# Moving weight stores and stage A's stores to the GpSimd queue, and dropping eight reloads of w_out

## The chip, the cores and the metric

The kernel runs on one core of a Trainium2 chip. The metric is the device time of one execution in microseconds (us). Engines are named as the profile names them: PE is TensorE, DVE is VectorE, ACT is ScalarE, POOL is GpSimd, and SP is SyncE, which here does nothing but issue DMA transfers. POOL, too, does nothing in this kernel but issue DMAs, apart from four tiny constants at the start.

## The reference

The input `x` has 8 batches of 3008 positions and 256 features, in float32. The first half is a real Fourier transform along the 3008 positions, a complex 256 by 256 mixing matrix with a bias, a soft threshold (lambda 0.01) and the inverse transform. The second half is a gated feed-forward layer on the resulting 24064 tokens, 256 to 2048 to 256 features.

```python
X = np.fft.rfft(x, axis=1)
Yr = Xr @ w_r - Xi @ w_i + b_r ;  Yi = Xr @ w_i + Xi @ w_r + b_i
Y = sign(Y) * max(|Y| - 0.01, 0)          # real and imaginary part apart
y = np.fft.irfft(Y, n=3008, axis=1)
h = y @ w_in ;  g = h * sigmoid(1.702 * h) ;  out = g @ w_out
```

[...]

## The kernel before

**The transform.** 3008 is 64 times 47, so each transform is done in two stages of small matrix products, stage A over 47 points and stage B over 64, joined through scratch tensors in device memory (`s1`, `s2`). For each batch, stage A has 16 steps: load a strip of `x` (line 325, tiles `xa` or `xr`), one matmul (line 342), ACT copies the result out of PSUM into a tile `aev` (line 357), and a DMA stores it to `s1` (line 358). Stage B has 12 steps: load from `s1` (lines 370 and 371, `kr` and `br`), matmuls (388), the mixing products (402 to 407), bias and threshold on DVE and ACT, four small transfers that regroup the result (427, `yr<-mv`), the inverse product (434), a copy (436, `iev`) and a store to `s2` (437). Tokens are then read back (467, `ur`) and transposed into `y` by a last product (475). Batch 0 runs first and alone. Batches 1 and 2 run their stage A as filler between the first steps of the feed-forward layer; from batch 3 on the transform of a batch is paced along it.

**The feed-forward layer.** Tokens go in 24 tiles (22 of 1024, then 2 of 768), each through 8 blocks of 256 hidden units; one tile and one block make a step, numbered n. A float32 product is three PE passes over a high and a low half (lines 147 to 149, `mm3`), made by `split` (line 144: an ACT copy and a DVE subtraction). The products are done in a Strassen scheme with seven products instead of eight: the up-projection from the start, the down-projection from the third tile on (n = 16). The first two tiles use plain `w_out` blocks (`wo`).

**The weights.** `fetch` (line 215, POOL's queue) loads a 512 KB float64 block. `from_float64` turns it into a float32 `a` and a float32 remainder `e`, with two ACT instructions (lines 230 and 234) and five DVE instructions (231, 232, 233, 235, 236). For the plain blocks, `turn(0, q)` splits that into the pair `wo[q][:, 0]` and `wo[q][:, 1]` (lines 254 to 256). `combine` (lines 259 to 276) makes the seven Strassen factors of a block. `keep` (lines 278 to 288) stores the finished factors to scratch tensors (`kept`, `kept_o`, `kept_d`), from which every later tile reloads them: `wq<-kept` at line 298, `wd<-kept_d` at line 652.

The eight Strassen factors of `w_out` are made in the steps n = 5 to 12. Each of these steps fetches the raw block of `w_out` a second time and converts it a second time, because the first conversion has been split by then.

**What sets the order.** The code is traced in program order; a planner then simulates the engines and decides the order of each engine's instructions and the reuse of buffers. Each engine works through its own list in order, so an instruction that waits holds up everything behind it on that engine or DMA queue. `tc.issue_after` puts an instruction behind a given one on the same engine. Buffers come in rings: tag `g` (13 slots) holds `xa`, raw weights, the converted pair `wae` and the factors `w`; tag `w2` (7 slots) holds `aev`, `xr`, `br`, `iev`, `mv` and most `ur`. A load into a ring slot waits until the slot's last user is done; for a slot that held `aev` that is the landing of its store.

Of the kernel before, what the change touches and what calls it, by code (L numbers as in the profile page):

```python
# [9 lines left out]
F32 = mybir.dt.float32  # L10
# [102 lines left out]
def fourier_mix_then_gated_ffn(ctx: ExitStack, tc: tile.TileContext, x, w_r, w_i, b_r, b_i, w_in, w_out, pack, kbs, out):  # L113
    nc = tc.nc
# [78 lines left out]
    kept = [dw.tile([128, 2 * NP * 128], F32, name=f"kept{q}") for q in range(NQ)]  # L193
    kept_o = [dw.tile([128, 4 * 256], F32, name=f"kept_o{q}") for q in range(NQ)]
    kept_d = [dw.tile([128, NP, 2, NQ // 2, 128], F32, name=f"kept_d{h}") for h in range(2)]
    up_w, wo, fresh = {}, {}, []
# [16 lines left out]
    def fetch(kind, q):  # L213
        raws[kind, q] = r = slot4([128, 2, 256], I64, "wraw")
        nc.gpsimd.dma_start(r, source(kind, q))

    def from_float64(kind, q):
        if (kind, q) not in raws:
            fetch(kind, q)
        raw = raws.pop((kind, q))  # L220
        ae = slot4([128, 2, 2, 256], I32, "wae")
        a, e = ae[:, 0], ae[:, 1]
        m = buf([128, 2, 256], F32, "wm", tag="s", bufs=3)
        af, ef = a.bitcast(F32), e.bitcast(F32)
        v = nc.vector

        def word(dt, w):
            return raw.bitcast(dt).rearrange("p c (f w) -> p c f w", w=2)[:, :, :, w]

        nc.scalar.activation(ef, word(F32, 1), AF.Abs)  # L230
        v.tensor_scalar(ef, ef, TINY, None, ALU.max)
        v.tensor_scalar(a, e, 3, 0x3FFFFFF8, ALU.logical_shift_left, ALU.bitwise_and)
        v.scalar_tensor_tensor(a, word(I32, 1), -0x40000000, a, ALU.bitwise_and, ALU.bitwise_or)
        nc.scalar.activation(m, word(U32, 0), AF.Copy, scale=2.0 ** -52)
        v.tensor_scalar(e, a, -0x800000, None, ALU.bitwise_and)
        v.tensor_tensor(ef, ef, m, ALU.mult)
        return af, ef
# [21 lines left out]
    def combine(kind, q, a, e, wq):  # L259
        a, e = (t.rearrange("p c (f n) -> p c f n", f=2) for t in (a, e))  # L260
        v = nc.vector
        t = slot4([128, 8, 128], F32, "w8")
        a11, a12, s4, n22, s1, s2, s3, a21 = (t[:, i] for i in range(8))
        v.tensor_tensor(t[:, 0:2], e[:, :, 0], a[:, :, 0], ALU.add)
        v.tensor_tensor(a21, e[:, 0, 1], a[:, 0, 1], ALU.add)
        v.scalar_tensor_tensor(n22, e[:, 1, 1], -1.0, a[:, 1, 1], ALU.mult, ALU.subtract)
        v.tensor_tensor(s1, a21, n22, ALU.subtract)
        v.tensor_tensor(s3, a21, a11, ALU.subtract)
        v.tensor_tensor(s2, s1, a11, ALU.subtract)
        v.tensor_tensor(s4, a12, s2, ALU.subtract)  # L270
        if kind:
            split(wq[:, 0], wq[:, 1], t[:, 0:7])
        else:
            wq = [slot4([128, NP, 128], F32R, "wq_d") for _ in range(2)]
            split(*wq, t[:, 0:7])
        fresh.append((kind, q, wq))

    def keep(n):
        for kind, q, wq in [f for f in fresh if f[0] != 1 or f[1] <= n]:
            fresh.remove((kind, q, wq))  # L280
            with tc.issue_after(stored[-1]):
                if kind == 1:
                    nc.sync.dma_start(kept[q], wq.bitcast(F32).rearrange("p h a n -> p (h a n)"))
                elif kind == 2:
                    nc.sync.dma_start(kept_o[q], wq.bitcast(F32).rearrange("p h f n -> p (h f n)"))
                else:
                    for h in range(2):
                        nc.sync.dma_start(kept_d[q // 4][:, :, h, q % 4], wq[h].bitcast(F32))

    def load_wo(q):  # L290
        wo[q] = buf([128, 2, 2, 256], F32R, "wo", tag="wd", bufs=WD)
# [12 lines left out]
    def spectral(b, s2):  # L304
# [34 lines left out]
        def stage_a(q):  # L339

            ps = bank()
            ins = nc.tensor.matmul(ps[:96], lhsT=ka32, rhs=xs.pop(q), start=True, stop=True).ins  # L342
            if plain_a:
                done_a.append(ins)
            if plain and q < 4:
                if q == 0:
                    shared.append(buf([96, 4, 512], F32, "aev_y", tag="y", bufs=1))
                ev = shared[0][:, q]
            elif plain and q < 7:
                if q == 4:  # L350
                    shared.append(buf([96, 3, 512], F32, "aev_t", tag="gl", bufs=JIT))
                ev = shared[1][:, q - 4]
            elif plain and q < 11:
                ev = buf([96, 512], F32, "aev_s", tag="s", bufs=3)
            else:
                ev = buf2("aev")[:96].rearrange("p j d -> p (j d)")
            evacuated.append(nc.scalar.copy(ev, ps[:96]).ins)
            mine.append(nc.sync.dma_start(s1w[:, 512 * q:512 * (q + 1)], ev).ins)
            stored.append(mine[-1])

        def load_b(sp):
# [466 lines left out]
    for n in range(NT * NQ):  # L828
        k, q = divmod(n, NQ)
        load_up(n + 2)  # L830
        last = q == NQ - 1 and k + 1 < NT
        if last:
            coming = Tile(k + 1)
        starts = list(np.cumsum((0,) + groups(k)))
        if k < PLAIN:
            group = None
        elif q in starts:
            group = (Group if k + 1 < NT else PlainGroup)(cur, q, groups(k)[starts.index(q)])
        if n == NQ * PLAIN + 1:
            wo.clear()  # L840
        step = Step(cur, q, group)

        if not queue and nextb < NB:
            if nextb == 2:
                queue = queue2
            else:
                first, second, *_ = spectral(nextb, new_s2(nextb))
                queue = first + [(4000, lambda: None)] + second
            nextb += 1
            total = None  # L850
        if queue and total is None and not filler:
            total, spent, n0 = sum(c for c, _ in queue), 0.0, n
            n1 = NQ * S * (nextb - 1) // TILE - 9
        for i, p in enumerate(PATTERN + (0,) * (k < PLAIN)):
            if p:
                step.up(p)
                if last:
                    coming.factor(p)
            elif behind:
                behind.pop(0)()  # L860
            else:
                for _ in range(2 if k + 1 == NT and q >= 4 else 1):
                    down()
            if i == 0 and n + EARLY < NQ:
                fetch(0, EARLY + n)
            if i == 4 and n + EARLY < NQ:
                with tc.issue_after(gelu[-1]):
                    turn(0, EARLY + n)
            if i == 5 and n + WQ < NQ:
                fetch(1, WQ + n)  # L870
            if i == 9 and n + WQ < NQ:
                with tc.issue_after(gelu[-1]):
                    turn(1, WQ + n)
            q2 = (n - 5) if 5 <= n < 5 + NQ else None
            if i == 0 and q2 is not None:
                fetch(0, q2)
            if i == 9 and q2 is not None:
                with tc.issue_after(gelu[-1]):
                    combine(0, q2, *from_float64(0, q2), None)
            if i % 5 == 2:  # L880
                fill(2)
                if i in (2, 12):
                    keep(n if i == 2 else -1)
                if preload_b and len(filler) <= 12:
                    preload_b()
                    preload_b = None
            part = n + (i + 1) / len(PATTERN)
            while queue and total and spent < total * (part - n0) / (n1 - n0):
                c, do = queue.pop(0)
                spent += c  # L890
                do()
            need = base[k + 1] + (base[min(k + 2, NT)] - base[k + 1]) * min(1.0, max(0.0, (part - NQ * k - 2.5) / 4))
            if JP * done < need:
                while queue and need + JP > S * (nextb - 1):
                    queue.pop(0)[1]()
                tokens_to(need)
        for do in behind:
            do()
        behind = []
        if group is None:  # L900
            behind = [lambda f=f, h=h, m=m, step=step: step.down(f, h, m) for f, h in BLOCKS for m in range(2)]
        elif q + 1 == group.q0 + group.n:
            preps += group.preps
            muls += group.muls
            group.load(0)
            group.load(1)
            prepare(used + JIT - 1)
        if last:
            cur = coming
            next_y()  # L910
# [38 lines left out]
```

## Time and profile before

| | |
|---|---|
| Median of 3 runs | 2559.37 us (2557.23 to 2566.39) |
| Profiled execution: time, span | 2557.47 us, 2555.5 us |
| PE busy | 2478.6 us, 97% of the span |
| DVE busy, ACT busy | 2051.7 us (80%), 1880.9 us (74%) |
| POOL busy | 14.8 us, 24 instructions, 20 of them DMAs |
| DMA traffic | 562.65 MB, mean 220 GB/s |
| SP's DMA queue, POOL's DMA queue | 549.77 MB, 10.49 MB |
| Chain that ended last, by engine | PE 86%, DMA 7%, DVE 4%, ACT 2% |
| Stores of stage A (line 358) | 128, of which batch 0 makes 16 |
| Stores of `keep` | 8 `kept`, 8 `kept_o`, 16 `kept_d` |

The span is the time from the first to the last instruction of the profiled execution. A busy PE is PE with matmuls in flight. The granted clock (PEclk) is 1.00 at TensorE's upper level, 2.4 GHz, and 0.50 at its lower level, 1.2 GHz; a value between them is the mean of a stretch. The view of stretches gives, for each, its length and the busy time of PE, PEld (weight loads), DVE, ACT and POOL with instruction counts, then the mean granted clock, the busy share of the DMA engines and what they moved. The waits view names, for an engine, the line that waited and what released it. The chain of waits goes back from the last instruction, at each step to what released it.

### The profile page before, as it was taken

How to read it: one execution, taken by the hardware profiler on the slowest of the kernel's cores; microseconds unless marked ns; L12 is line 12 of the kernel's file. 1: busy time of each engine (PE TensorE's matmuls, PEld its weight loads, DVE VectorE, ACT ScalarE, POOL GpSimd, SP SyncE). 2: the span in 40 equal slices, each digit the busy share in tenths (PEclk: the TensorE clock that was granted, in tenths of full speed). 3: DMA queues.
4: the chain of work that ended last, by engine and by line, in shares of the span. 5: the costliest groups of instructions: out<-in, count | busy, mean ns of one | idle time of the engine just before them, and what ended most of it. 6: DMA issues, size and time to landing. Idle time of an engine off the chain costs nothing.

```text
span 2555.5 us, 35590 instructions
## 1 busy us (share of the span) xinstructions
PE 2478.6 (97%) x12270; PEld 2055.6 (80%) x12270; DVE 2051.7 (80%) x2627; ACT 1880.9 (74%) x3025; POOL 14.8 (1%) x24
## 2 busy tenths in 40 slices
PE   8889899999999999999999999999999999999998
PEld 5557787888788887888868887788877888888888
DVE  4568775988789887898878987788878988888984
ACT  4467666877778778777777777777777777887775
POOL 0000000000000000000000000000000000000000
PEclk9889999999999999999999999999999999999999
DMA  7777675666876668766786667766686676765564
GB/s 242 240 241 241 202 216 191 199 221 211 258 230 199 224 220 258 236 198 218 226 257 203 213 211 256 237 210 219 199 285 218 210 224 202 238 202 198 181 225 150
DMA packets 259298, 562.65 MB, mean 220 GB/s; under 512 B 28881, under 2 KB 143825, under 8 KB 259121
## 3 DMA queue, kind: packets, MB, share of 16 engines
q1 hardware_dynamic: 256080, 549.77, 66.8%
q0 software_dynamic: 2880, 10.49, 1.4%
q8 instruction: 99, 1.62, 0.3%
q14 instruction: 79, 0.64, 0.1%
q10 hardware_dynamic: 160, 0.13, 0.0%
HBM read 441.26 MB, written 93.85 MB: 209 GB/s over the span
## 4 chain that ended last, share of the span: by engine, by line
PE 86%; DMA 7%; DVE 4%; ACT 2%; issue 1%; SPq 1%; ACTq 0%; DVEq 0%
PE pa L147 12%; PE pa L148 12%; PE pa L149 12%; PE po L147 10%; PE po L148 10%; PE po L149 10%; PE pa L475 4%; PE pa L342 4%; PE pa L388 3%; PE pa L434 3%; PE seed L147 2%; PE seed L149 2%; PE seed L148 2%; DMA wq<-kept 1%; DMA xr<-in_x 1%; DMA xa<-in_x 1%
## 5 line engine op out<-in xcount | busy, mean ns | idle before, releaser
L144 DVE TENSOR_TENSOR gl<-g,gl 128x1024 fp32r<-128x1024 f32 (+3 forms) x672 | 762.9, 1144 | 190.3 <-ACT gl L144 187.7
L144 ACT CAST gl<-g 128x1024 fp32r<-128x1024 f32 (+3 forms) x672 | 659.1, 991 | 164.7 <-PE po L149 144.3
L147 PE MATMUL pa<-tk,wq 128*128 128x512 f32 (+1 forms) x1169 | 492.8, 423 | 16.6 <-DMA wq<-kept 6.0
L147 PE MATMUL po<-gl,wd 128*128 128x512 f32 (+1 forms) x1176 | 465.4, 402 | 3.4 <-DVE pt L535 3.0
L148 PE MATMUL po<-gl,wd 128*128 128x512 f32 (+1 forms) x1176 | 463.3, 394 | 0.2 <-DVE gl L144 0.2
L149 PE MATMUL po<-gl,wd 128*128 128x512 f32 (+1 forms) x1176 | 458.1, 390 | 0.0
L148 PE MATMUL pa<-tk,wq 128*128 128x512 f32 (+1 forms) x1169 | 455.1, 389 | 0.0
L149 PE MATMUL pa<-tk,wq 128*128 128x512 f32 (+1 forms) x1169 | 451.9, 388 | 0.0
L659 DVE TENSOR_TENSOR g<-g 128x1024 f32<-128x1024 f32 (+1 forms) x336 | 401.5, 1205 | 11.4 <-ACT g L579 10.0
L578 DVE TENSOR_TENSOR g<-pa,s 128x512 f32<-128x512 f32 (+1 forms) x401 | 268.7, 674 | 92.0 <-PE pa L149 59.8
L572 ACT COPY s<-pa 128x512 f32<-128x512 f32 (+1 forms) x401 | 230.7, 577 | 98.2 <-PE pa L149 93.4
L147 PEld LDWEIGHTS pa<-tk,wq 128*128 128x128 f32 x1169 | 221.9, 190 | 75.6 <-ACT s L572 12.3
L579 ACT ACTIVATE g<-g 128x512 f32<-128x512 f32 (+1 forms) x401 | 248.8, 623 | 39.1 <-DVE g L578 38.0
L147 PEld LDWEIGHTS po<-gl,wd 128*128 128x128 f32 x1176 | 220.7, 188 | 51.5 <-DVE pt L535 4.4
L148 PEld LDWEIGHTS po<-gl,wd 128*128 128x128 f32 x1176 | 221.4, 188 | 47.1 <-issue 4.2
L149 PEld LDWEIGHTS po<-gl,wd 128*128 128x128 f32 x1176 | 221.2, 188 | 46.0 <-issue 2.5
L149 PEld LDWEIGHTS pa<-tk,wq 128*128 128x128 f32 x1169 | 221.0, 189 | 44.9 <-issue 0.2
L148 PEld LDWEIGHTS pa<-tk,wq 128*128 128x128 f32 x1169 | 222.0, 190 | 43.0 <-issue 10.1
L535 DVE TENSOR_TENSOR pt<-po,pt 128x512 f32<-128x512 f32 (+1 forms) x210 | 142.2, 677 | 20.3 <-PE po L149 20.0
L475 PEld LDWEIGHTS pa<-kc,ur 96*128 96x128 f32 x1024 | 136.1, 191 | 16.4 <-issue 3.7
L147 PE MATMUL pa<-wf_h,zt 128*128 128x256 f32 x504 | 143.2, 284 | 0.2 <-ACT iev L436 0.2
L144 DVE TENSOR_TENSOR tk<-y,tk 128x512 fp32r<-128x512 f32 (+1 forms) x168 | 110.6, 673 | 40.7 <-ACT tk L144 40.5
(112 smaller groups left out, 3435.5 us busy)
## 6 DMA issues: line engine op xcount, KB each, us to landing
wq<-kept SPq DMA_DIRECT2D x184, 896.0 KB, 5.3
wd<-kept_d SPq DMA_DIRECT2D x294, 512.0 KB, 4.1
br<-s SPq DMA_DIRECT2D x96, 256.0 KB, 4.4
s<-iev SPq DMA_DIRECT2D x96, 256.0 KB, 3.5
ur<-s SPq DMA_DIRECT2D x128, 192.0 KB, 4.8
yr<-mv SPq DMA_DIRECT2D x382, 64.0 KB, 3.2
out<-pt SPq DMA_DIRECT2D x88, 256.0 KB, 4.3
s<-aev SPq DMA_DIRECT2D x117, 192.0 KB, 3.9
```

The lines of the kernel that those rows point to most:

```text
L144: return nc.scalar.copy(hi, src).ins, nc.vector.tensor_tensor(lo, src, hi.bitcast(F32), ALU.subtract).ins
L147: nc.tensor.matmul(ps, lhsT=wh, rhs=xh, start=start, stop=False, skip_group_check=more)
L148: nc.tensor.matmul(ps, lhsT=wh, rhs=xl, start=False, stop=False, skip_group_check=more)
L149: nc.tensor.matmul(ps, lhsT=wl, rhs=xh, start=False, stop=stop, skip_group_check=more)
L342: ins = nc.tensor.matmul(ps[:96], lhsT=ka32, rhs=xs.pop(q), start=True, stop=True).ins
L388: nc.tensor.matmul(pv[:, c, :, i], lhsT=t[:, i, cs], rhs=k[:, i], start=True, stop=True)
L475: turned.append(nc.tensor.matmul(pv[:, c, 94 * j:94 * j + 94], lhsT=t[:, j, 128 * c:128 * c + 128], rhs=kz, start=True, stop=True).ins)
L535: nc.vector.tensor_tensor(t, ps[:, :w], t, ALU.add)
L572: nc.scalar.copy(t, ps[:, :self.w])
L578: nc.vector.tensor_tensor(t, ps[:, :w], self.s[other], ALU.add)
L579: gelu[:] = (nc.scalar.activation(t, ps[:, :w] if other is None else t, AF.Gelu_apprx_sigmoid).ins,)
L659: nc.vector.tensor_tensor(out, x, y, ALU.subtract)
```

## The change

Three edits. The stores of `keep` go out from POOL's queue and no longer from SP's. The stores of stage A do so too for every batch but batch 0 (`plain` is true for batch 0 alone). And in the steps n = 5 to 12 the second fetch and conversion of a `w_out` block is gone: `combine` reads the two halves of `wo[q2]`, which lie in SBUF already, as `a` and `e`.

```diff
 def keep(n):
             with tc.issue_after(stored[-1]):
                 if kind == 1:
-                    nc.sync.dma_start(kept[q], ...)
+                    nc.gpsimd.dma_start(kept[q], ...)
                 elif kind == 2:
-                    nc.sync.dma_start(kept_o[q], ...)
+                    nc.gpsimd.dma_start(kept_o[q], ...)
                 else:
                     for h in range(2):
-                        nc.sync.dma_start(kept_d[q // 4][:, :, h, q % 4], wq[h].bitcast(F32))
+                        nc.gpsimd.dma_start(kept_d[q // 4][:, :, h, q % 4], wq[h].bitcast(F32))
...
-            mine.append(nc.sync.dma_start(s1w[:, 512 * q:512 * (q + 1)], ev).ins)
+            mine.append((nc.sync if plain else nc.gpsimd).dma_start(s1w[:, 512 * q:512 * (q + 1)], ev).ins)
...
             q2 = (n - 5) if 5 <= n < 5 + NQ else None
-            if i == 0 and q2 is not None:
-                fetch(0, q2)
             if i == 9 and q2 is not None:
                 with tc.issue_after(gelu[-1]):
-                    combine(0, q2, *from_float64(0, q2), None)
+                    combine(0, q2, wo[q2][:, 0].bitcast(F32), wo[q2][:, 1].bitcast(F32), None)
```

## Rows read from the trace of the kernel before

**Rows 1.** Busy times by stretch: PE, PEld, DVE, ACT, POOL; PEclk, DMA share, GB/s.

```profile
95.00:220.00 125.00, 107.61 (x381) 67.11 (x380) 72.01 (x139) 74.78 (x137) 7.95 (x11) 0.88 0.75 255
220.00:365.00 145.00, 134.04 (x739) 115.15 (x739) 121.63 (x237) 98.33 (x175) 5.06 (x7) 0.96 0.67 210
420.00:2300.00 1880.00, 1869.27 (x9344) 1557.68 (x9343) 1576.95 (x1845) 1452.06 (x2279) 0.00 (x0) 1.00 0.70 223
```

**Rows 2.** PE's waits, 95 to 220 us: total us, times, longest.

```profile
PE pa L342 <- DMA xa<-in_x: 7.4, 5, 3.0
```

**Rows 3.** PE's waits, 220 to 365 us.

```profile
PE pa L388 <- ACT iev L436: 7.3, 1, 7.3
```

**Rows 4.** PE's waits, 420 to 2300 us.

```profile
PE pa L342 <- DMA xr<-in_x: 5.3, 4, 2.5
```

**Rows 5.** Waits of SP's DMA queue, 95 to 220 us.

```profile
SPq L358 <- ACT aev L357: 56.6, 22, 10.7
```

**Rows 6.** Waits of SP's DMA queue, 420 to 2300 us.

```profile
SPq L358 <- ACT aev L357: 66.4, 44, 5.0
SPq L325 <- DMA s<-aev: 48.6, 20, 7.9
```

**Rows 7.** The chain of waits, 95 to 220 us: start, us, what.

```profile
117.75 5.69 DMA xa<-in_x
...
140.96 4.26 DMA xa<-in_x
...
166.58 0.42 SPq L283
167.09 6.89 DMA xa<-in_x
...
189.14 6.10 DMA xa<-in_x
...
205.19 3.55 DMA xa<-in_x
```

**Rows 8.** The chain of waits, 220 to 365 us.

```profile
255.83 0.42 DVE wae L235
...
275.50 0.55 SPq L288
...
276.81 5.84 DMA yr<-mv
...
360.85 0.57 ACT wm L234
```

**Rows 9.** The conversion's instructions by line: ns min/median/max, first and last start us.

```profile
L230 ACT ACTIVATE wae<-wraw x24: 642/670/700, 23.5 to 360.2; 128x512 f32<-128x512 f32 x24
L231 DVE TENSOR_SCALAR wae<-wae x24: 415/422/429, 24.3 to 361.1; 128x512 f32<-128x512 f32 x24
L232 DVE TENSOR_SCALAR wae<-wae x24: 416/427/430, 24.7 to 361.6; 128x512 int32<-128x512 int32 x24
L233 DVE SCALAR_TENSOR_TENSOR wae<-wraw,wae x24: 680/692/700, 25.2 to 362.1; 128x512 int32<-128x512 int32 x24
L234 ACT ACTIVATE wm<-wraw x24: 651/666/689, 24.1 to 360.8; 128x512 f32<-128x512 uint32 x24
L235 DVE TENSOR_SCALAR wae<-wae x24: 406/421/427, 25.9 to 364.3; 128x512 int32<-128x512 int32 x24
L236 DVE TENSOR_TENSOR wae<-wae,wm x24: 680/686/694, 26.4 to 365.2; 128x512 f32<-128x512 f32 x24
```

**Rows 10.** Two DMA-issuing lines, POOL's and SP's: ns min/median/max of an issue.

```profile
L215 POOL DMA_DIRECT2D wraw<-in_w_out x15: 722/722/838, 79.0 to 330.0; - x15
L358 SPq DMA_DIRECT2D s<-aev x117: 303/311/1416, 21.6 to 1935.4; - x117
```

**Rows 11.** DMA issues: count, KB each, median us from issue to landing.

```profile
wraw<-in_w_out POOLq DMA_DIRECT2D x15, 512.0 KB, 5.7
wraw<-in_w_in SPq DMA_DIRECT2D x3, 512.0 KB, 7.8
```

More of the change, by code (lines that the diff above doesn't have):

```diff
@@ L282, in keep @@
                 if kind == 1:
-                    nc.sync.dma_start(kept[q], wq.bitcast(F32).rearrange("p h a n -> p (h a n)"))
+                    nc.gpsimd.dma_start(kept[q], wq.bitcast(F32).rearrange("p h a n -> p (h a n)"))
                 elif kind == 2:
-                    nc.sync.dma_start(kept_o[q], wq.bitcast(F32).rearrange("p h f n -> p (h f n)"))
+                    nc.gpsimd.dma_start(kept_o[q], wq.bitcast(F32).rearrange("p h f n -> p (h f n)"))
                 else:
                     for h in range(2):
-                        nc.sync.dma_start(kept_d[q // 4][:, :, h, q % 4], wq[h].bitcast(F32))
+                        nc.gpsimd.dma_start(kept_d[q // 4][:, :, h, q % 4], wq[h].bitcast(F32))
     def load_wo(q):
```

## The prediction

> **What bounds the kernel now.** I read the page's busy shares first, then the busy times by stretch, then the waits of PE and of SP's queue in each stretch, and last the chain of waits of the opening. The busy shares say PE (97%); the stretches say where that is not so. From 420 to 2300 us PE is busy 1869.3 of 1880 us at a granted clock of 1.00, so all that any edit could win there is 10.7 us [rows 1]. The opening is different. From 95 to 220 us PE is idle 17.4 of 125 us, and its granted clock is 0.88, which costs as much as 0.12 x 125 = 15.0 us at the upper level. From 220 to 365 us it is idle 11.0 of 145 us, and at 0.96 the clock costs another 5.8 us. Together 28.4 us of idle time and 20.8 us of clock [rows 1]. The tail after 2300 us is touched by none of the edits.
>
> What ends PE's waits differs between the two parts. From 95 to 220 us it is first of all the loads of `x` for stage A: 7.4 us in 5 waits [rows 2]. On the chain these five loads stand with 5.69, 4.26, 6.89, 6.10 and 3.55 us [rows 7], and the third of them has a weight store of `keep` (line 283) issued directly ahead of it. SP's queue itself spends 56.6 us of this stretch at line 358, waiting for ACT to finish an `aev` whose store is next in the list [rows 5]; any `xa` load behind that store waits too. From 220 to 365 us the largest PE wait is 7.3 us, once, for an `iev` copy [rows 3]. The chain before it runs through the conversion's DVE instructions, a `kept_d` store on SP (0.55 us) and the `yr<-mv` transfers behind it (5.84 us) [rows 8].
>
> **The change part by part.**
>
> *The dropped reloads.* Eight fetches of 512 KB and eight conversions go. A conversion is five DVE instructions, 0.422 + 0.427 + 0.692 + 0.421 + 0.686 = 2.65 us, and two on ACT, 0.670 + 0.666 = 1.34 us [rows 9]; eight of them 21.2 us of DVE and 10.7 us of ACT. `combine` itself stays. Most of this lies beside PE, for PE is busy 134 of these 145 us while DVE is busy 121.6 [rows 1]. What lay on the path is what the chain shows: seven pieces of the conversion from 255.83 us (0.42) to 360.85 us (0.57), together 3.6 us [rows 8]. The bounds are 0, if the work next in line is just as late, and 16.8 us, all idle time and clock loss of the stretch. I take 3.6, since the rows of the chain are the nearest. If a stall here goes, `yr<-mv` and the threshold on DVE are late next; they are not touched.
>
> *The stores of `keep` on POOL.* All 32 leave SP. For the `kept_d` stores the chain prices one at 0.55 us, in front of `yr<-mv` [rows 8]; the bound is the 7.3 us of the wait that those transfers end [rows 3]; I take 1.5 us, as SP also waits in front of such stores for the factors to be finished. The other 16 stores belong to the next item.
>
> *Stage A's stores on POOL, 95 to 220 us.* SP no longer waits for `aev` at its head, and an `xa` load no longer stands behind a weight store in the same queue. The loads can only go as early as their ring slots are free. The least is 0, the most is 7.4 us of direct waits [rows 2], and with the idle time and clock around them the 32.4 us of the stretch. I take 5.0 of the 7.4: the third to fifth load keep some wait for a slot. Behind a load that comes earlier, ACT's copies are late next.
>
> *Clock.* Fewer gaps should leave PE less long at 1.2 GHz. The bounds are 0 and 20.8 us [rows 1]; the terms above take 10.1 of 28.4 us of idle time, and in proportion that would be 7.4 us. I take a third of it, 2.4 us, because the gaps that I fill are short ones.
>
> *What POOL's queue costs.* An issue takes 0.722 us on POOL against 0.311 us on SP [rows 10], so a store starts some 0.41 us later once its `aev` is ready. 112 stores move; if each delay reached PE that would be 46 us. If only those did whose loads PE waits for today, 5 early and 4 late ones [rows 2, 4], it would be 3.7 us. Below nothing: 36 of the 80 later stores found SP somewhere else when their `aev` was ready (80 less 44) [rows 6], and these go out sooner; that can win at most the 5.3 us of rows 4. In the opening the stores also share POOL with 11 fetches that wait for slots of ring `g`, and behind a waiting fetch stand stores, behind them `aev` slots, and behind these ACT's next `aev` copy. I take 3.0 us of cost in all, near the 3.7. From 420 to 2300 us I take no gain: SP's 66.4 us of waits for `aev` mostly become waits for the same store's landing at the next `xr` load, which is in the list already with 48.6 us in 20 waits [rows 6].
>
> The sum: 3.6 + 1.5 + 5.0 + 2.4 - 3.0 = 9.5 us, from the profiled execution's 2557.5 us to 2548.0 us. That execution lies 1.9 us below the median of 2559.4, inside the spread of the three runs; against the median the forecast is 0.45% less.
>
> The row on issue speaks for POOL's transfers in one respect: the same kind of 512 KB block landed 5.7 us after its issue on POOL and 7.8 us on SP [rows 11], though at different times. The Trainium skill, page "DMA: Bandwidth & Descriptors", section "Issuing engines are not separate DMA queues", speaks against the change: all transfers run on the same 16 DMA engines whoever issues them, and a second issuer saves only the sequencer's issuing time. It leaves out that an issuer waits in order, which is what rows 5 show. By that rule the third item would be worth next to nothing; that is a rival below.
>
> **The rivals.**
>
> *Only the issue time is saved (that rule).* The `xa` loads wait for slots and for DMA engines that are busy 0.75 of the stretch [rows 1], not for SP's place in the list. Then the third item gives nothing, the clock little, and 3.6 + 1.5 - 3.0 leaves 2.1 us: 2555.4 us. For it speaks the DMA share; against it the 56.6 us at SP's head [rows 5].
>
> *The opening closes up.* Loads, `kept_d` stores and conversions were the only things late, and PE's clock stays up: half of the 28.4 + 20.8 us comes back, some 25 us: 2533 us. For it speaks that PE's idle time in the opening has several causes, of which all the large ones are touched; against it that DVE is busy 84% from 220 to 365 us and loses only a sixth of that.
>
> *The store becomes the late link (slower).* A load of `xr` into a slot that held `aev` waits for that store to land: 20 times today, 2.4 us each [rows 6]. On POOL each store starts 0.41 us later, in bursts of stage A the delay passes from store to load to matmul to the next store, and a fetch at POOL's head adds to it in the opening. If 80 stores pass on 0.41 us, that is 33 us, less the gains of 10.1 us: 2580 us; with half of the stores it is 2564. It beats the median from about 30 stores on. For it speaks that ring `w2` has only 7 slots; against it that PE waits for `xr` only 4 times in 1880 us [rows 4].
>
> **How the numbers follow.** The forecast (2540 to 2553 us) gets 0.43, the saving of issue time alone 0.20, the closed opening 0.15, the late store 0.22. A measurement of this kernel tells about 0.5% from no change, 12.8 us, so faster means below 2546.6 us and slower above 2572.2 us. Of the forecast 0.20 lies below the first line and 0.23 above it; with the closed opening, faster has 0.35. The late store gives 0.17 to slower and 0.05 to no change, which with the 0.23 and the 0.20 makes 0.48. The range runs from 2531 us, past the closed opening, to 2573 us, where most of the milder half of the late store lies; the forecast alone would have 2540 to 2556.
>
> **What would show it.** The lines 230 to 236 must stand with 16 instructions each and POOL's fetches with 12. Right: SP's waits for `aev` at line 358 gone after the first batch, PE's waits for `xa` below 3 us, PE idle less than 20 us from 95 to 365 us at a clock above 0.88 and 0.96, PE in the long middle as before. Wrong on the third item: `xa` waits as long, with SP now waiting at line 325 for slots. Wrong on POOL's cost: ACT held at line 357 by stores that haven't landed, or PE's waits for `xr` above 15 us. Since the planner orders every engine's list anew, a shift of PE's order that changes the long middle by over 10 us would also make the sum wrong.

## The result, and the profile after

The changed kernel takes 2537.24 us (median of 4 runs, 2536.25 to 2540.75) against 2560.3 us for the kernel before (2557.23 to 2566.39): a ratio of 0.9902, 95% interval 0.9884 to 0.9920, so 23 us by the medians, 25 us by the ratio, about 1.0% faster. The forecast was 2548.0 us, a gain of 9.5 us; the measured one is more than twice that, inside the stated range. The profiled execution took 2537.07 us with a span of 2534.9 us, 20.4 us less than the profiled execution before.

A mark that lies at the same place of the work in every kernel shows where: the load of `wq` (line 298) that is issued on SP for step 8, 12 and 24. From the timeline of SP's queue, the kernel before (start us, us, what):

```profile
232.52 1.04 SPq L298 DMA_DIRECT2D wq<-kept  x1
...
308.31 0.66 SPq L298 DMA_DIRECT2D wq<-kept  x1
...
469.84 0.32 SPq L298 DMA_DIRECT2D wq<-kept  x1
```

and the changed kernel:

```profile
227.09 0.71 SPq L298 DMA_DIRECT2D wq<-kept  x1
...
288.39 0.33 SPq L298 DMA_DIRECT2D wq<-kept  x1
...
450.17 0.32 SPq L298 DMA_DIRECT2D wq<-kept  x1
```

Up to step 8 the changed kernel wins 5.4 us, from step 8 to 12 another 14.5, up to step 24 it stands at 19.7, and all the rest of the run adds 0.9 (the spans differ by 20.6). The gain is made in the opening, and most of it in the steps that had the reloads. Between the loads for step 8 and step 24 the traces hold the same work for PE, 1188 matmuls before and 1185 after: PE's idle time there fell from 16.2 to 5.7 us and its busy time from 221.1 to 217.4 us, as the granted clock rose from 0.98 to 1.00. Busy times between these two marks, before and after:

```profile
232.52:469.84 237.32, 221.13 (x1188) 187.68 (x1186) 178.40 (x313) 161.52 (x283) 4.34 (x6) 0.98 0.65 202
```

```profile
227.09:450.17 223.08, 217.39 (x1185) 185.50 (x1184) 158.03 (x265) 152.89 (x267) 14.83 (x17) 1.00 0.63 201
```

The busy times of the same stretches as in [rows 1], and PE's waits from 95 to 220 us, from 220 to 365 us and from 420 to 2300 us, of the changed kernel:

```profile
95.00:220.00 125.00, 107.57 (x410) 70.82 (x411) 78.07 (x153) 78.33 (x144) 33.63 (x58) 0.92 0.78 267
220.00:365.00 145.00, 140.52 (x775) 120.04 (x774) 105.54 (x200) 95.39 (x167) 14.83 (x17) 1.00 0.63 197
420.00:2300.00 1880.00, 1873.17 (x9333) 1560.73 (x9332) 1583.81 (x1854) 1458.40 (x2285) 41.10 (x80) 1.00 0.68 223
```

```profile
PE po L147 <- ACT gl L144: 9.5, 5, 4.8
...
PE pa L342 <- DMA xa<-in_x: 1.4, 1, 1.4
```

```profile
PE pa L434 <- DVE g L578: 1.7, 1, 1.7
```

```profile
PE pa L342 <- DMA xr<-in_x: 3.7, 3, 2.6
```

From 220 to 365 us PE's idle time fell from 11.0 to 4.5 us and the granted clock rose from 0.96 to 1.00; the wait of 7.3 us [rows 3] is gone. From 95 to 220 us the loads of `xa` keep PE waiting 1.4 us and not 7.4 [rows 2], but PE is idle 17.4 us as before, since its waits for ACT's `gl` grew from 4.5 to 9.5 us; the clock is 0.92 and not 0.88. The waits for `xr` went from 5.3 to 3.7 us [rows 4].

The stores on POOL, by line (ns min/median/max of an issue, first and last start), and by DMA issue (KB, median us to landing):

```profile
L358 POOL DMA_DIRECT2D s<-aev x112: 514/514/546, 98.9 to 1912.8; - x112
```

```profile
s<-aev POOLq DMA_DIRECT2D x112, 192.0 KB, 4.0
...
kept_d<-wq_d POOLq DMA_DIRECT2D x16, 448.0 KB, 7.4
```

An issue takes 0.51 us and not the 0.72 us that a fetch took [rows 10].

### The profile page after: what moved, and what is told of

It reads as the page before. It is cut to its first block, busy times and chain, and to the rows that moved or that the text cites. A ratio compares the mean times of both kernels' runs of the same rounds, so it can differ in the third digit from the quotient of the medians.

```text
span 2534.9 us, 35670 instructions
## 1 busy us (share of the span) xinstructions
PE 2472.7 (98%) x12270; PEld 2056.0 (81%) x12270; DVE 2032.7 (80%) x2587; ACT 1872.5 (74%) x3009; POOL 90.6 (4%) x160
## 4 chain that ended last, share of the span: by engine, by line
PE 89%; DMA 5%; DVE 3%; ACT 2%; issue 1%; SPq 0%; POOL 0%; ACTq 0%; DVEq 0%; POOLq 0%
PE pa L147 12%; PE pa L148 12%; PE pa L149 12%; PE po L147 11%; PE po L148 11%; PE po L149 11%; PE pa L475 4%; PE pa L342 4%; PE pa L388 3%; PE pa L434 3%; PE seed L147 2%; PE seed L149 2%; PE seed L148 2%; PE pa L405 1%; DMA s<-iev 1%
## 5 line engine op out<-in xcount | busy, mean ns | idle before, releaser
L659 DVE TENSOR_TENSOR g<-g 128x1024 f32<-128x1024 f32 (+1 forms) x336 | 402.1, 1206 | 12.2 <-ACT g L579 10.8
L147 PEld LDWEIGHTS po<-gl,wd 128*128 128x128 f32 x1176 | 221.7, 189 | 52.7 <-DVE pt L535 5.0
L147 PE MATMUL pa<-wf_h,zt 128*128 128x256 f32 x504 | 142.8, 283 | 0.2 <-ACT iev L436 0.2
L149 PE MATMUL pa<-wf_h,zt 128*128 128x256 f32 x504 | 142.3, 282 | 0.0
```

The costliest lines, as they stand in the source:

```text
L147: nc.tensor.matmul(ps, lhsT=wh, rhs=xh, start=start, stop=False, skip_group_check=more)
L149: nc.tensor.matmul(ps, lhsT=wl, rhs=xh, start=False, stop=stop, skip_group_check=more)
L659: nc.vector.tensor_tensor(out, x, y, ALU.subtract)
```

## The experiments

Below, "ratio" is to the kernel before on the same chip, with the 95% interval; 0.001 is 2.6 us. "To step 8" and "8 to 24" come from the marks above, one profiled execution each, so they carry a few us of scatter. The kernel before had a median of 2560.3 us in the first comparison and of 2564.9 to 2569.5 us in those of the experiments, so whole times are compared by the ratio alone. "Pinned" says whether `issue_after(stored[-1])` in `keep` still binds.

| kernel | reloads | keep's stores | A's stores | ratio | to step 8, us | 8 to 24, us |
|---|---|---|---|---|---|---|
| before | yes | SP, pinned | SP | 1 | 232.5 | 237.3 |
| changed | no | POOL, pinned | POOL | 0.9902 (0.9884 to 0.9920) | 227.1 | 223.1 |
| e1 | no | SP, pinned | SP | 0.9926 (0.9905 to 0.9948) | 236.4 | 223.3 |
| e2 | yes | POOL, loose | SP | 1.0063 (1.0044 to 1.0082) | 243.0 | 250.7 |
| e3 | yes | SP, loose | POOL | 0.9994 (0.9980 to 1.0008) | 239.5 | 238.4 |
| e5 | no | POOL, loose | SP | 0.9950 (0.9932 to 0.9969) | 241.9 | 222.1 |
| e6 | no | SP, loose | POOL | 0.9944 (0.9929 to 0.9958) | 239.4 | 221.7 |
| e7 | yes | POOL, pinned | POOL | 1.0038 (1.0024 to 1.0053) | 231.2 | 261.9 |
| e9 | no | SP, pinned to `xa` | POOL | 0.9898 (0.9878 to 0.9918) | 229.4 | 219.7 |
| e10 | no | POOL, loose | POOL | 0.9929 (0.9901 to 0.9957) | 232.6 | 222.0 |

**The parts by themselves (e1 to e3).** Each applies one hunk of the diff to the kernel before: e1 the last, e2 the three lines of `keep`, e3 the line of stage A.

```diff
-                    combine(0, q2, *from_float64(0, q2), None)      # e1, and no fetch(0, q2)
+                    combine(0, q2, wo[q2][:, 0].bitcast(F32), wo[q2][:, 1].bitcast(F32), None)
...
-  nc.sync.dma_start(kept[q], ...)          # e2, kept_o and kept_d likewise
+  nc.gpsimd.dma_start(kept[q], ...)
...
-  mine.append(nc.sync.dma_start(...))      # e3
+  mine.append((nc.sync if plain else nc.gpsimd).dma_start(...))
```

> Only the dropped reloads: combine reads wo[q2], all stores stay on SP. Theory 1 (the time came from the 21.2 us of DVE and 10.7 us of ACT work taken out of 220 to 365 us, which fed the one long PE gap there): 12 to 18 us faster than before, the gap of 7.3 us at line 388 gone, granted clock 1.00 from 220 to 365 us. Theory 2 (it came from SP's queue, where yr<-mv no longer stands behind kept_d stores): 0 to 5 us faster, the gap stays. Theory 3 (the planner's new order of PE is what counts, the edits are not): any number, not related to the part.

> Only the 32 stores of keep move to POOL's queue; reloads and stage A's stores as before. Theory 1: 0 to 5 us faster. Theory 2: 10 to 18 us faster, the wait of 7.3 us at line 388 gone. Theory 3: any number.

> Only the 112 stores of stage A move to POOL's queue. The prediction had 5 us less wait for xa and 3 us of cost: with theory 1 or 2, within 4 us of before, PE's waits for xa from 95 to 220 us down from 7.4 to under 3 us, but PE's idle time there nearly as before. Theory 3: any number.

Theory 2 fell: alone, the stores of `keep` on POOL cost 16 us and do not win 10. Dropping the reloads wins 19 us, just above the 12 to 18 of theory 1, and its marks are there in e1 (the wait of 7.3 us gone, a clock of 1.00 from 220 to 365 us); that the engine work is the cause does not follow, and e8 and e11 below speak against it. Stage A's stores change nothing measurable; PE no longer waits for `xa` in e3, but for `ur` (4.6 us) and ACT's `s` (6.1 us) instead. The three parts sum to a gain of 4 us; together they gain 23. So they act on one another.

POOL's timeline of e2 shows one way in which they do:

```profile
286.30 0.90 POOL L288 DMA_DIRECT2D kept_d<-wq_d  x1 [26.10 <-ACT wq_d L144]
287.03 0.91 POOL L215 DMA_DIRECT2D wraw<-in_w_out  x1
287.74 1.15 POOL L288 DMA_DIRECT2D kept_d<-wq_d  x1
303.69 0.90 POOL L288 DMA_DIRECT2D kept_d<-wq_d  x1 [14.80 <-ACT wq_d L144]
304.42 0.92 POOL L215 DMA_DIRECT2D wraw<-in_w_out  x1
305.40 0.92 POOL L288 DMA_DIRECT2D kept_d<-wq_d  x1
```

The bracket is POOL's idle time and what ended it. Each fetch stands directly behind a `kept_d` store that waits for ACT to finish the factors of the block before. The next block's load begins only then, so the conversions run one after the other with the load's full time in between: ACT waits for `wraw` 15.9 us in 6 waits (220 to 420 us), where the kernel before has none.

**The pairs (e5 to e7).** The same hunks, two at a time.

> Dropped reloads and the stores of keep on POOL; stage A's stores stay on SP. Theory of the queue (keep's stores alone cost 16 us because on POOL each reload's fetch stood behind a kept_d store that waited for the factors before it; with the reloads gone nothing stands behind them): 18 to 28 us faster than before, no more than 6 us from the changed kernel. Rival, effects add (0.9926 and 1.0063): 3 us faster.

> Dropped reloads and stage A's stores on POOL; the stores of keep stay on SP. Effects add: 20 us faster than before. Theory of the queue: 15 to 22 us faster, as the dropped reloads alone; kept_d stores still in front of yr<-mv on SP cost under 5 us.

> All stores on POOL, the reloads kept. Theory of the queue: 10 to 25 us slower than before, since the fetches of the reloads still stand behind kept_d stores. Theory of SP's relief (the stores in front of yr<-mv were what counted, and stage A's stores help keep's): 5 us or more faster.

The theory of the queue holds for the steps 8 to 24: 250.7 and 261.9 us where reloads and POOL stores meet (e2, e7), 222 us without reloads (e5). But e5 gains 13 us and not 18 to 28, and e6 with 14 and e7 with 10 us of loss lie at the edge of what was expected. The table shows what it lacks: e2, e3, e5 and e6 all reach step 8 late, at 239 to 243 us. They are the kernels in which only one kind of store moved. That does not give SP a free head, it puts one wait in the place of another: from 95 to 235 us SP waits 64 us for `aev` at line 358 in e5, 60 us for finished factors at lines 283 and 285 in e6, and at none of these lines in the changed kernel. `keep` puts its stores behind stage A's last store, and that binds on one engine only; with the two kinds on different queues the stores of `keep` drift to an early place in their list and wait at its head. SP's waits in e6, 95 to 235 us (1 us at these lines in e1, where the pin holds):

```profile
SPq L285 <- DVE wo L256: 36.1, 6, 18.6
SPq L283 <- DVE wq L144: 23.5, 4, 9.1
```

**The pin (e9, e10).** e9 is e6 with another anchor, e10 the changed kernel without one.

```diff
-            with tc.issue_after(stored[-1]):        # keep, e9
+            with tc.issue_after(strips[-1]):        # strips: load_x's transfers, on SP
...
-            with tc.issue_after(stored[-1]):        # keep, e10
+            if True:
```

> As e6 (dropped reloads, stage A's stores on POOL, the stores of keep on SP), but keep's stores are put behind the last xa load with issue_after; with stage A's stores on POOL the old anchor stands on another engine and binds nothing. Theory of the pin (the two moves cost singly because keep's stores lost their place and waited at the head of the queue for factors that were not made yet; moved together they keep it): 19 to 27 us faster than before (ratio 0.9895 to 0.9925), SP's waits at lines 283 and 285 from 95 to 235 us down from 60 us to under 15 us, the load of wq for n = 8 at 226 to 232 us. Rival (only the planner's order of PE differs): as e6, 0.9944, give or take the 0.0036 that a change of order alone gave.

> The changed kernel with one thing undone: keep's stores are no longer put behind stage A's last store, so they stand earlier in POOL's list. Theory of the pin: 8 to 18 us slower than the changed kernel (ratio to before 0.9940 to 0.9975), with POOL waiting at lines 283 and 285 from 95 to 235 us for some 60 us or more and the time lost before the load of wq for n = 8. Rival (order only): 0.9902, give or take 0.0036.

e9 brings back the whole loss of e6 (the intervals lie apart) and reaches step 8 at 229.4 us, as expected; SP's waits at lines 283 and 285 fell from 60 to 30 us, less than expected:

```profile
SPq L285 <- DVE wo L256: 20.7, 6, 13.4
SPq L283 <- DVE wq L144: 6.4, 1, 6.4
SPq L283 <- DMA ur<-s: 2.3, 1, 2.3
```

e10 went the expected way, 5.5 us later at step 8, but by less than expected, and its interval overlaps the changed kernel's, so e10 doesn't decide between the pin and the order: POOL waited at line 285 only 23 us and at 283 not at all. Where the loose stores did wait on POOL, in e2 and e5 (121 us at these lines from 95 to 235 us, with fetches behind them), step 8 came latest of all.

**What in a reload costs (e8, e11, e17).** All three drop the reloads and put one piece back that nobody reads; stores stay on SP as in e1.

```diff
+                fetch(0, q2)                                        # e8: 512 KB into ring g
...
+                    raws[0, q2] = held_raw; from_float64(0, q2)     # e11: conversion of one held block
...
+                nc.gpsimd.dma_start(r[:, 0, 0:8], source(0, q2)[:, 0, 0:8])   # e17: 8 KB, same slot
```

> As the dropped reloads alone, but the eight fetches of 512 KB stay (their tiles are read by nobody); all stores on SP. If DVE's and ACT's conversion work was the cost: as the dropped reloads, 14 to 22 us faster. If the DMA traffic or the slots of ring g that the raw blocks take were the cost: within 5 us of before.

> The eight conversions stay on DVE and ACT, but seven of the eight fetches go (all eight convert the first block, and their result is read by nobody; combine reads wo); all stores on SP. The dropped reloads gave 19 us and the conversions alone dropped 9 us. If fetch and conversion share the cost: 5 to 14 us faster than before. If the fetches were the smaller part and only the wait of combine for its block counted: 14 us or more faster. If DVE's and ACT's time is all: within 5 us of before.

> As e8 (reloads dropped, but a raw tile is still taken from ring g in each of the eight steps and filled by a DMA on POOL that nobody reads), with 8 KB per fetch and not 512 KB. If the traffic was the cost of the fetches: as e1, a ratio to before of 0.990 to 0.9945, and 221 to 225 us from the load of wq for step 8 to that for step 24. If the slot was: as e8, 0.995 to 0.998, and 229 to 234 us.

| | fetch | conversion | ratio | 8 to 24, us |
|---|---|---|---|---|
| before | 512 KB | yes | 1 | 237.3 |
| e8 | 512 KB | no | 0.9964 (0.9950 to 0.9978) | 231.8 |
| e11 | one only | yes, unread | 0.9937 (0.9914 to 0.9960) | 223.6 |
| e17 | 8 KB | no | 0.9925 (0.9902 to 0.9948) | 221.9 |
| e1 | none | no | 0.9926 (0.9905 to 0.9948) | 223.3 |

The raw block's slot and the issue on POOL cost nothing (e17 equals e1). By this one pair the 512 KB cost 10 us: the edits of e8 and e17 differ in little else, and their intervals lie just apart, though the planner orders PE's matmuls anew here too, nearly as much as in the neutral changes below. The 21 us of DVE and 11 us of ACT work, run beside the rest, cost 0.3 us by the marks and 3 by the ratio, where the intervals of e11 and e1 overlap; so this work is not the price. What is left of the 19 us, some 6, would be the path through a reload, fetch, conversion, combine, store, which neither e8 nor e11 has; that is a subtraction, no run shows it by itself. In e8 and e17 the bytes tell on the transfers that a step of stage B waits for. DMA issues from 220 to 365 us, e8 and then e17:

```profile
yr<-mv SPq DMA_DIRECT2D x40, 64.0 KB, 3.2
...
s<-iev SPq DMA_DIRECT2D x7, 256.0 KB, 5.3
```

```profile
yr<-mv SPq DMA_DIRECT2D x44, 64.0 KB, 2.8
...
s<-iev SPq DMA_DIRECT2D x8, 256.0 KB, 3.2
```

Over all the runs the landing of `yr<-mv` follows the fetches only in part. Its median in this stretch is 3.2 to 4.3 us in the kernels with eight full fetches and SP for the stores of `keep` (before, e3, e4, e8, e13, e15) and 2.0 to 2.8 us in those without them, but also 2.0 and 2.1 us in e7 and e2, which have the fetches and are the slowest; and `s<-iev` took 3.3 us in the kernel before, no longer than in e17.

**The planner's order (e4, e12 to e16).** These change only where `combine`, with the fetch and conversion that belong to it, is called, for the kernel before and the changed one. The planner lists PE's work otherwise each time: in the traces some hundred of its matmuls stand in another place.

```diff
-            if i == 9 and q2 is not None:           # e4, e12: i == 8;  e13, e14: i == 12
...
-            q2 = (n - 5) if 5 <= n < 5 + NQ else None
+            q2 = (n - 6) if 6 <= n < 6 + NQ else None     # e15, e16
```

> A change of order alone: combine of the eight blocks is called one place earlier in each step (i = 8 and not 9); same work, same queues, but the planner gives PE a list that differs in some hundred places. Theories 1 and 2: within 4 us of before. Theory 3: it moves by 8 us or more either way.

> The changed kernel with the change of order of e4 (combine at i = 8): same work and queues. If the planner's order is worth some 9 us at random, the ratio to before lies anywhere from 0.986 to 0.994; if the changed kernel's gain is made by the queues and the dropped work, within 0.0020 of 0.9902. It could also be the faster version.

> The kernel before with combine three places later in its step (i = 12): same work and queues, another order on PE. If the order is worth some 9 us at random: a ratio to before anywhere from 0.994 to 1.006.

> The changed kernel with combine at i = 12. If the edits make the gain: 15 to 27 us faster than e13. If the order makes most of it: 0 to 10 us faster than e13.

> The kernel before with the eight combines, fetches and conversions a whole step later (n = 6 to 13): same work and queues. Order at random: 0.994 to 1.006.

> The changed kernel with the eight combines a whole step later. If the edits make the gain: 15 to 27 us faster than e15. If the order makes most of it: 0 to 10 us faster than e15.

| place of combine | before's work | changed kernel's work | difference |
|---|---|---|---|
| i = 9 | 1 | 0.9902 | 0.0098 |
| i = 8 (e4, e12) | 0.9964 (0.9949 to 0.9980) | 0.9954 (0.9933 to 0.9975) | 0.0010 |
| i = 12 (e13, e14) | 0.9984 (0.9967 to 1.0000) | 0.9882 (0.9862 to 0.9903) | 0.0102 |
| a step later (e15, e16) | 1.0015 (0.9996 to 1.0034) | 0.9930 (0.9909 to 0.9952) | 0.0085 |

The order alone moves the kernel by up to 9 us before and 13 us after the change. Still, in three of four orders the edits gain 22 to 26 us; the mean of the four is 0.0074, 19 us. e12 with 0.9954 lies outside both ranges named for it, and e4's 9 us are what theory 3 asked for. It follows, too, that a difference of some 10 us between two single kernels, as of e8 and e17 or of e6 and e9, could by itself be the order's; what speaks for the causes given is that the landing times (e8 and e17) and the waits (e6 and e9) moved with them.

For the dropped reloads as a whole the marks show more, since they do so in several orders. From step 8 to 24 the five kernels that fetch and convert again, with the stores of `keep` on SP (before, e3, e4, e13, e15), take 235 to 238 us; ten of the twelve whose `combine` reads `wo` (changed, e1, e5, e6, e9, e10, e11, e14, e16, e17) take 217 to 227 us, whatever the order and the queues. PE is idle 11 to 16 us there in the five, at a clock of 0.97 or 0.98, and 2 to 9 us in the ten, at 0.99 or 1.00. The two others are e8 with its fetches (231.8 us) and e12 (237.1 us). That the stores on POOL add anything to this is not shown: the mean of the changed kernel's four orders is 0.9917, and e1, with all stores on SP, has 0.9926.

In e12 the changed kernel keeps its lead until step 11 and loses 14 us of it up to step 24; the stretch 280 to 400 us, e12 and then the changed kernel:

```profile
280.00:400.00 120.00, 105.91 (x546) 88.84 (x545) 61.49 (x110) 63.20 (x113) 7.08 (x8) 0.94 0.58 183
```

```profile
280.00:400.00 120.00, 114.56 (x612) 96.07 (x611) 71.68 (x125) 73.30 (x132) 7.09 (x8) 1.00 0.61 194
```

PE is idle 14.1 us and not 5.4, and the clock is 0.94 for most of the same work. Which line of the list starts it stays open. The fastest version tried is e14, 0.9882; its interval overlaps those of the changed kernel and of e9.

## Why the prediction was right and wrong

The size was not right (9.5 us forecast, 23 measured); the sign, the place and most of the marks were: 16 conversions and 12 fetches on POOL, SP's waits for `aev` gone, `xa` waits under 3 us, both clocks up, the long middle unmoved. One mark failed narrowly, PE's idle time from 95 to 365 us: 21.9 us, not below 20.

*The dropped reloads, 3.6 us: this step failed.* It priced a reload by the pieces of its conversion that lay on the chain, and its fetch at nothing. Alone the reloads are worth 19 us (e1, 13 to 24 by the interval), and the conversions as engine time at most a few of these (e11). The fetched bytes are 10 us by the pair e8 and e17, a size that an order alone also made (e12), so how the 19 divide between the bytes and the path through a reload stays open. The chain did point to the bytes: its `yr<-mv` of 5.84 us in the middle of the stall [rows 8] was a 64 KB transfer, and the median for these from 220 to 365 us fell from 3.7 us before to 2.0 after (but it is 2.0 in e7 too, which keeps the fetches). The single wait of 7.3 us [rows 3] was not the price: e4, e13 and e15, the kernel before in other orders, have no wait of PE above 5.1 us from 220 to 400 us and still need 235 to 238 us from step 8 to 24. The bound given, 16.8 us for the stretch with its clock, held for the 14.5 us between steps 8 and 12; e1's 19 us lie above it, though its interval takes it in.

*The clock, 2.4 us: too small.* Reckoned as in the prediction, the two stretches regained 5.0 and 5.8 us of clock [rows 1], 10.8 us in all, but a stretch of fixed length holds other work after the change. For the whole run, with 12,270 matmuls each, PE's busy time fell by 5.9 us, from 2478.6 to 2472.7 us, and its idle time by 14.7 us. The long stall sat in front of matmuls at the lower level (the granted clock of the kernel before was 0.50 from 280 to 288 us); when it went, the stretch ran at 1.00. A proportion of idle time, and then a third of that, was no basis.

*Keep's stores, 1.5 us, and stage A's stores, 5.0 us.* Neither wins anything alone (e2, e3). Up to step 8 the changed kernel wins 5.4 us, near the forecast (6.5, less 3.0 of cost), but that is partly luck: e7, which moves both and keeps the reloads, wins 1.3 us there, and e14, the changed kernel in another order, none. The working had not seen a condition, too: moved singly the stores lose `issue_after`, and step 8 comes 7 to 10 us late (4 us in e1, where nothing moved). e9 shows that the stores of `keep` need not leave SP at all.

*POOL's cost, 3.0 us: not seen.* The issue is 0.20 us longer, not 0.41, and the landing is 4.0 us as against 3.9. The real cost of POOL was elsewhere, a fetch behind a `kept_d` store (e2, e7), and the dropped reloads remove just that.

Of the rivals, the late store did not come. That only issue time is saved fits e3, where the third item gave nothing, but e9 against e1 (0.9898 and 0.9926, overlapping) leaves room for a few us. The closed opening (2533 us, given 0.15) came nearest, but not for the reason named, that the large causes of PE's idle time were all touched: e1 touches only the reloads and has 19 us. That the result lies inside the stated range is owed to this rival at its lower end; the forecast's own, 2540 to 2556 us, lies above it.

## What to carry to other kernels

Price a dropped reload by the whole path through it, the fetch, the conversion and what waits for them, and by PE's idle time and clock around it, not by the pieces of engine work that one chain shows. Its bytes may count by what they do to small transfers beside them (10 us in the one pair tried here). When DMAs move to another queue, look at what is pinned to them: an order edge that binds on one engine is lost without a word if one end moves (SP's waits at lines 283 and 285 went from 1 to 60 us), and a transfer that waits at the head of its new queue holds up whatever stands behind it. Where a planner makes the order, a difference of half a per cent between two versions means little until a neutral change of order has been timed beside it.

## What the runs showed that was not expected

POOL's issue time goes with the shape: 0.514 us for a store of `aev` (96 by 512), 0.89 us for one of `kept_d` (128 by 896, in pieces of 128); SP's were 0.311 and 0.561 us in the kernel before. The `kept_d` stores took 7.4 us to land from POOL and 3.6 us from SP before, while those of `aev` took 4.0 and 3.9 us. The queue alone does not explain the 7.4: in other kernels they took 5.4 us (e1) and 7.3 us (e8) from SP, and 5.0 us from POOL (e14).
